# Stage one of the six last batches of an FFT mixing layer: split float32r products in place of float32 ones

## The chip, the cores and the metric

The kernel runs on one core of a Trainium2 chip. The metric is the device time of one execution in microseconds (us). A NeuronCore has five engines with a queue of instructions each: TensorE (PE, with its weight loads as PEld), VectorE (DVE), ScalarE (ACT), GpSimd (POOL) and SyncE (SP), which here issues most of the DMAs. An engine takes its queue in order; semaphores make it wait for other engines and for DMAs.

## What is computed

`x` has 8 batches of 3008 positions with 256 channels. A real FFT runs over the positions, the spectrum is mixed over the channels with a complex weight matrix and a bias, shrunk softly, and transformed back. A feed-forward block with 2048 hidden units and a squared ReLU follows. All of it is float32.

```python
X = np.fft.rfft(x, axis=1)
Yr = Xr @ w_r - Xi @ w_i + b_r
Yi = Xr @ w_i + Xi @ w_r + b_i
Yr = np.sign(Yr) * np.maximum(np.abs(Yr) - lam, 0.0)      # Yi likewise
y = np.fft.irfft(Yr + 1j * Yi, n=3008, axis=1)
h = np.maximum(y @ w_in, 0.0)
out = (h * h) @ w_out
```

## The kernel before

3008 is 64 x 47, so the FFT is done in two stages. Stage one is a transform of length 47 for each of 64 residues, with the 47 inputs folded into 24 sums and 24 differences: a product with the constant matrix `am32` (120 x 2 x 120), which serves five residues at a time. Thirteen steps of this kind make up a batch, and their results go to memory in `s1`. Stage two and the mixing (class `Pair`), the transform back (`Pair.back`, `Back`) and the feed-forward block (`Tokens`, `Step`) follow.

In the main loop, slot after slot, the feed-forward block of batch `b` runs as the backbone: tiles of about 500 positions, eight `Step`s a tile, two slots a `Step`. Each `Step` makes seven products into `psh` (21 matmuls of 250 columns), lets DVE and ACT turn them into `c`, rounds that to float32r on ACT and forms the rest on POOL (`mg`, two halves), and multiplies `mg` with `wout` into `pso` (two times six matmuls of 500 columns). All of these stand at line 478, the line of a helper (`then`) that ties them into one order on each engine. Beside it run the pairs of batch `b + 1` and stage one of batch `b + 2`, as jobs with a due slot: `fwd_tasks` gives a `Fwd` step every 7 slots (6 in the first round). Its load is due 2.5 slots ahead of the step, `add` 0.8 ahead and `run` 0.3 after.

A `Fwd` step loads `xt` (line 209, two buffers), folds it into `xs` by two POOL instructions (lines 212 and 227, one buffer), and `run` (line 232) multiplies: two float32 products of `am32` with 256 columns (line 235), an ACT copy into `xe`, and a store. This is how batches 2 to 7 go, six of them, 78 steps. Batch 0 is done by `Fwd32` at the start (line 367) and batch 1 by `Fwd2` (line 346), which needs no folds but a third weight matrix, `nam`, the negative of half of `am32`.

`halves(hi, lo, v, eng)` is the helper of every split: `hi` is `v` rounded to float32r by a copy on ACT (line 97), `lo` the rest `v - hi` in float32r, subtracted on `eng` (line 101). A product of two split operands is three float32r matmuls: high by high, low by high, high by low, as in `Pair.mul` (line 300).

Tiles are taken by name with a number of buffers from `FRONT` and `MAIN`, two where neither says otherwise. A new tile waits for all readers of the one whose buffer it takes. `SIDE` lists the tiles that lie in the memory that becomes free once the weights are converted, in slot 5. The order of the instructions of an engine is not that of the program: it is laid out ahead of the run from expected times, with the due slots as the order of preference; `issue_after` ties one instruction behind another. `load_next` chains the loads of `xt`, `ka`, `kb` and `du` on SP in this way.

Of the kernel before, what the change touches and what calls it, by code (L numbers as in the profile page):

```python
# [9 lines left out]
F32 = mybir.dt.float32  # L10
F32R = mybir.dt.float32r
# [12 lines left out]
B, S, D, FF = 8, 3008, 256, 2048  # L24
# [4 lines left out]
M1 = R * G  # L29
# [8 lines left out]
}  # L38
MAIN = {
    "xs": 1, "xe": 1, "du": 1, "kv": 1, "kp": 1, "kq": 1, "ksh": 1, "ksl": 1, "kxl": 1, "kb": 1, "yr": 1,  # L40
    "ms": 1, "mp": 1, "mu": 1, "mv": 1, "mc": 3, "nam": 1,
}
CONV = ("big", "small", "dw", "ds")
SIDE = ("xs", "ka", "kb", "kcm", "kxh", "kxl", "kp", "kq", "ke", "kv", "ksh", "ksl", "kuh", "kul", "ku")

# [11 lines left out]
def fnet_moe(ctx: ExitStack, tc, x, w_r, w_i, b_r, b_i, w_in, w_out, bm, cm, dx, a32, c32, out):  # L59
    nc = tc.nc  # L60
    pe, act, dve, pool = nc.tensor, nc.scalar, nc.vector, nc.gpsimd
# [7 lines left out]
    am32 = const.tile([M1, 2, M1], F32, name="am32")  # L69
# [11 lines left out]
    def memory(stack, name, **kwargs):  # L81
        return stack.enter_context(tc.tile_pool(name=name, bufs=2, reuse_waits="tile", **kwargs))
# [5 lines left out]
    def T(name, shape, dt, tag=None):  # L88
        tag = tag or name
        return pools.get(tag, phase["pool"]).tile(shape, dt, name=name, tag=tag, bufs=phase["bufs"].get(tag, 2))  # L90

    def bank(shape, name="psf"):
        return phase["psum"].tile(shape, F32, name=name, tag=name, bufs=phase["bufs"].get(name, 1))

    def copy(eng, out, in_):
        if eng is act:
            return act.copy(out=out, in_=in_)  # L97
        return eng.tensor_copy(out=out, in_=in_)  # L98

    def sub(eng, out, a, b):  # L100
        return eng.tensor_tensor(out=out, in0=a, in1=b, op=ALU.subtract)  # L101
# [65 lines left out]
    def halves(hi, lo, v, eng):  # L167
        copy(act, hi, v)
        sub(eng, lo, v, hi)
# [33 lines left out]
    class Fwd:  # L203
# [19 lines left out]
            )  # L223
            return nc.sync.dma_start(dst, self.ev[:, :n])


        def add(self):
            self.u = T("xs", [M1, 2, D], F32)
            for t in range(2):
                self.fold(pool, self.u[:, t:t + 1], t)  # L230

        def run(self):
            ps = bank([128, 2, D])
            for t in range(2):
                nc.tensor.matmul(ps[:M1, t], am32[:, t], self.u[:, t], start=True, stop=True)  # L235
            self.ev = T("xe", [M1, 1, 2, D], F32)
            copy(act, self.ev[:, 0], ps[:M1])
            self.store()
# [99 lines left out]
    class Fwd2(Fwd):  # L338
# [3 lines left out]
        def run(self):  # L342
            ps = bank([128, 2, D])
            for t in range(2):
                for i in range(2):
                    nc.tensor.matmul(  # L346
                        ps[:M1, t], nam if t and i else am32[:, t], self.xt[:, 0, i], start=i == 0, stop=i == 1
                    )
            self.ev = T("xe", [M1, 1, 2, D], F32)
            copy(act, self.ev[:, 0], ps[:M1])  # L350
            self.store()
# [230 lines left out]
    def pair_tasks(pairs, start, step):  # L582
        jobs = []
        for j, u in enumerate(pairs):
            at = start + j * step
            if j:
                jobs += [(at - 3.7, u.load)]
            jobs += [
                (at, u.fwd), (at + 1.0, u.sums), (at + 3.7, u.load_back),
                (at + 2.1, lambda u=u: u.mix(1)), (at + 3.0, lambda u=u: u.mix(0)), (at + 4.0, u.shrink),  # L590
                (at + 7.1, lambda u=u: u.back(0)), (at + 8.0, lambda u=u: u.back(1)),
            ]
        return jobs

    def fwd_tasks(b, start, step):
        jobs = []
        for q in range(J):
            f, at = Fwd(b, q), start + q * step
            jobs += [(at - 2.5, f.load), (at - 0.8, f.add), (at + 0.3, f.run)]
        return jobs  # L600

    def back_tasks(t, start):
        b, c0, h = tiles[t]
        new = range(-(-c0 // W2), -(-(c0 + 2 * h) // W2))
        jobs = []
        for j, q in enumerate(new):
            k, at = Back(b, q), start + 2.2 * j
            jobs += [(at, k.load), (at + 1.6, k.mm)]
            if len(k.spans) > 1:
                jobs += [(start + 14.6, k.put)]  # L610
        k = Tokens(t)
        for j in range(2):
            jobs += [(start + 7.1 + j, lambda j=j: k.sums(j))]
        for j in range(4):
            jobs += [(start + 9.1 + 1.2 * j, lambda j=j: k.split(j))]
        return jobs
# [24 lines left out]
    def convert(n, after=None):  # L641
        p = parts[n]
        p.bits(after)
        p.join()
        if n % 4 > 1:
            p.split()
        elif n % 4:
            win_sums(n // 4, parts[n - 1:n + 1])
# [10 lines left out]
    for r in range(-5, len(units) + 3):  # L659
# [20 lines left out]
        pool=memory(ctx, "main"), bufs={**{k: FRONT[k] for k in CONV}, **MAIN, "psf": 2}, psum=memory(ctx, "main_ps", space=PSUM)  # L680
# [9 lines left out]
                job()  # L690
    for n in range(len(parts) - LATE, min(LATER.values())):
        convert(n, units[-1])
    nam = T("nam", [M1, M1], F32)
    act.mul(nam, am32[:, 1], -1.0)
    second = [Fwd2(1, q) for q in range(J)]
    for q in range(3):
        second[q].load()
# [3 lines left out]
    for m in range(2 * len(steps) + 4):  # L701
        b, r = divmod(m, slots)
        if r == 0 and b < B:
            jobs = [(t - slots, job) for t, job in jobs]
            if b + 1 < B:
                first, step = 1.0, 6.1
                if b == 0:
                    first, step = 11.2, 5.5
                    for q in range(2, J):
                        if q > 2:  # L710
                            jobs += [(0.9 * (q - 3), second[q].load)]
                        jobs += [(0.5 + 0.9 * (q - 2), second[q].run)]
                    jobs += [(first - 0.6, pairs[1][0].load)]
                jobs += pair_tasks(pairs[b + 1], first, step)
            if b + 2 < B:
                first, step = (2.6, 7.0) if b else (14.6, 6.0)
                jobs += fwd_tasks(b + 2, first, step) + [(95.0, pairs[b + 2][0].load)]
            for j in range(len(HALF)):
                t = b * len(HALF) + j + 1
                if t < len(tiles):  # L720
                    jobs += back_tasks(t, NF * j + 0.5)
            jobs.sort(key=lambda j: j[0])
        n, k = divmod(m, 2)
        if k and 0 <= n - 2 < len(steps):
            steps[n - 2].out(1)
        if n < len(steps):
            (steps[n].second if k else steps[n].first)()
        if not k and 0 <= n - 2 < len(steps):
            steps[n - 2].out(0)
        if m in LATER:  # L730
            convert(LATER[m], steps[n])
        if m == max(LATER):
            conv.close()
            pools.update(dict.fromkeys(CONV), **dict.fromkeys(SIDE, memory(ctx, "side")))
        while jobs and jobs[0][0] < r + 1:
            jobs.pop(0)[1]()

# [85 lines left out]
```

## Time and profile before

| | us |
|---|---|
| median of 3 runs | 2632.47 |
| the runs | 2632.03 to 2634.69 |
| profiled execution | 2632.53 |
| its span | 2630.8 |
| TensorE busy | 2569.7 |
| VectorE busy | 1781.6 |
| ScalarE busy | 1670.4 |
| GpSimd busy | 1654.5 |

The profile is of one execution. The span goes from its first to its last instruction. The chain of waits is followed back from the last instruction, at each step to what released it. Durations of single matmuls overlap, since the engine starts one before the last has drained, so what a matmul costs is read from the pitch of a row of them in the chain.

### The profile page before, as it was taken

To read this page: it belongs to the slowest core of one execution; us is meant where nothing else is said; L and a number is where in the kernel's file an instruction comes from. 1 tells how busy PE (TensorE), PEld (TensorE's weight loads), DVE (VectorE), ACT (ScalarE), POOL (GpSimd) and SP (SyncE) were. 2 spreads that over 40 slices of the span, in tenths; PEclk is the share of its full clock that TensorE was granted. 3 is DMA by queue.
4 is the path that set the end of the run, shared out by engine and by line. 5 is a ranking of instruction groups with operands and counts; after the bars stand their busy time and mean duration, and the time that the engine had idled before them with its cause. 6 is when DMAs were issued, how large, how long until landed. Compare 5 with 4: busy or idle time off the path is not lost.

```text
span 2630.8 us, 47549 instructions
## 1 busy us (share of the span) xinstructions
PE 2569.7 (98%) x16908; PEld 2349.9 (89%) x16908; DVE 1781.6 (68%) x3797; ACT 1670.4 (63%) x2433; POOL 1654.5 (63%) x1628
## 2 busy tenths in 40 slices
PE   6798989999999999999999999999999999999999
PEld 4688989899999999999999999999999999999998
DVE  6866666676766667677675766767676677765554
ACT  3465656666666666666666666666666666666665
POOL 3245656766676667666675676667766666666564
PEclk8899999999999999999999999999999999999999
DMA  8642333333332333323332333223332223221100
GB/s 261 202 141 88 111 101 94 90 106 93 112 90 78 113 101 96 89 85 104 103 95 84 101 104 103 89 82 99 103 108 87 72 80 93 77 67 39 35 17 17
DMA packets 191455, 250.51 MB, mean 95 GB/s; under 512 B 21755, under 2 KB 135923, under 8 KB 191219
## 3 DMA queue, kind: packets, MB, share of 16 engines
q1 hardware_dynamic: 178915, 225.12, 28.0%
q0 software_dynamic: 12304, 22.35, 3.6%
q8 instruction: 136, 2.23, 0.4%
q14 instruction: 100, 0.82, 0.1%
HBM read 146.85 MB, written 100.53 MB: 94 GB/s over the span
## 4 chain that ended last, share of the span: by engine, by line
PE 91%; DMA 3%; DVE 3%; POOL 2%; ACT 1%; issue 1%; SPq 0%; POOLq 0%; ACTq 0%; DVEq 0%
PE pso L478 38%; PE psh L478 34%; PE psf L300 7%; PE psf L279 3%; PE psf L235 2%; PE psf L332 2%; PE psf L458 1%; PE psf L459 1%; PE psf L455 1%; DMA du<-s 1%; POOL mg L101 1%; PE psf L346 1%; PE psf L409 1%; DMA x<-x_in 0%; DMA s<-xe 0%
## 5 line engine op out<-in xcount | busy, mean ns | idle before, releaser
L101 POOL TENSOR_TENSOR mg<-mc,mg 128x500 fp32r<-128x500 f32 (+1 forms) x768 | 973.8, 1288 | 589.0 <-ACT mg L97 536.0
L478 PE MATMUL pso<-mg,wout 128*128 128x500 f32 (+1 forms) x4608 | 1178.0, 393 | 3.2 <-POOL mg L101 1.7
L478 PE MATMUL psh<-yt,win 128*128 128x250 f32 (+1 forms) x8064 | 1072.4, 281 | 0.0
L478 ACT ACTIVATE mc<-mc 128x1000 f32<-128x1000 f32 (+1 forms) x768 | 802.5, 1045 | 416.0 <-DVE mc L478 406.0
L478 PEld LDWEIGHTS psh<-yt,win 128*128 128x128 f32 x8064 | 1021.9, 189 | 31.8
L478 PEld LDWEIGHTS pso<-mg,wout 128*128 128x128 f32 x4608 | 819.8, 189 | 132.8 <-POOL mg L101 4.3
L478 DVE TENSOR_TENSOR mc<-psh,mv 128x500 f32<-128x500 f32 (+3 forms) x768 | 419.1, 547 | 439.7 <-PE psh L478 407.4
L97 ACT CAST mg<-mc 128x1000 fp32r<-128x1000 f32 (+1 forms) x384 | 396.9, 1034 | 18.2 <-ACT mc L478 0.4
L478 DVE TENSOR_TENSOR mv<-psh,mu 128x500 f32<-128x500 f32 (+1 forms) x384 | 260.6, 679 | 53.9 <-PE psh L478 22.9
L300 PE MATMUL psf<-wx,kxh 128*128 128x256 f32 x1008 | 208.0, 283 | 0.8 <-DVE ke L312 0.8
L98 DVE COPY mp<-psh 128x250 f32<-128x250 f32 (+1 forms) x384 | 159.6, 416 | 40.9 <-PE psh L478 18.6
L101 POOL TENSOR_TENSOR ksl<-kv,ksh 128x512 fp32r<-128x512 f32 x84 | 108.6, 1293 | 107.9 <-ACT ksh L97 107.9
L300 PEld LDWEIGHTS psf<-wx,kxh 128*128 128x128 f32 x1008 | 167.5, 190 | 4.9 <-DVE ke L312 1.3
L478 DVE TENSOR_TENSOR mu<-psh,mp 128x250 f32<-128x250 f32 (+1 forms) x384 | 160.6, 418 | 11.7
L214 POOL TENSOR_TENSOR xs<-xt 120x256 f32<-120x256 f32 x156 | 114.6, 754 | 84.9 <-DMA xt<-x_in 76.7
L321 DVE TENSOR_TENSOR kv<-psf,ke 64x256 f32<-64x256 f32 x336 | 141.8, 422 | 28.1 <-PE psf L300 20.0
L478 DVE TENSOR_TENSOR mc<-psh,mp 128x250 f32<-128x250 f32 (+1 forms) x384 | 156.8, 408 | 5.2 <-PE psh L478 3.6
L300 PE MATMUL psf<-wx,kxl 128*128 128x256 f32 x504 | 141.5, 281 | 0.0
L97 ACT CAST kuh<-psf 128x256 fp32r<-128x256 f32 x192 | 68.3, 372 | 99.5 <-PE psf L332 79.8
L97 ACT COPY dy<-psf 128x188 f32<-128x188 f32 x256 | 76.5, 312 | 86.5 <-PE psf L459 86.2
L312 DVE TENSOR_TENSOR ke<-psf,bias 128x512 f32<-128x512 f32 x84 | 58.0, 691 | 105.8 <-PE psf L300 105.5
L97 ACT CAST ksh<-kv 128x512 fp32r<-128x512 f32 x84 | 52.0, 619 | 114.5 <-DVE kv L101 114.3
(97 smaller groups left out, 2565.4 us busy)
## 6 DMA issues: line engine op xcount, KB each, us to landing
du<-s SPq DMA_DIRECT2D x128, 256.0 KB, 2.9
s<-kuh SPq DMA_DIRECT2D x192, 128.0 KB, 1.8
s<-kul SPq DMA_DIRECT2D x192, 128.0 KB, 1.9
s<-xe SPq DMA_DIRECT2D x92, 240.0 KB, 2.4
xt<-x_in SPq DMA_DIRECT2D x91, 240.0 KB, 3.4
kcm<-cm_in POOLq DMA_DIRECT2D x84, 256.0 KB, 3.3
ka<-s SPq DMA_DIRECT2D x84, 256.0 KB, 3.4
du<-s SPq DMA_DIRECT2D x256, 64.0 KB, 2.7
```

What stands on the lines that cost most here:

```text
L97: return act.copy(out=out, in_=in_)
L98: return eng.tensor_copy(out=out, in_=in_)
L101: return eng.tensor_tensor(out=out, in0=a, in1=b, op=ALU.subtract)
L214: return eng.tensor_tensor(out=out[:, :n], in0=self.xt[:, :n, 0], in1=self.xt[:, :n, 1], op=(ALU.add, ALU.subtract)[t])
L235: nc.tensor.matmul(ps[:M1, t], am32[:, t], self.u[:, t], start=True, stop=True)
L279: nc.tensor.matmul(pv[:, :, c, g, :], self.a[:, g, c * 128:(c + 1) * 128], bg, start=True, stop=True)
L300: self.last = nc.tensor.matmul(ps, l, wx[j][:, k, c, :], start=n == 0, stop=n == 5)
L312: dve.tensor_add(out=self.e, in0=self.pe, in1=bias)
L321: dve.tensor_add(out=v[64 * r:64 * r + 64, g], in0=ps[gs], in1=self.e[gs, r])
L332: nc.tensor.matmul(ps[:, :D], self.cm[:, g, j * 128:(j + 1) * 128], r[:, g], start=n == 0, stop=n == 2)
L346: nc.tensor.matmul(ps[:M1, t], nam if t and i else am32[:, t], self.xt[:, 0, i], start=i == 0, stop=i == 1)
L478: last_of[eng] = op(*args, **kwargs)
```

## The change

`Fwd.add` splits the folded sums `u` into `uh` and `ul` by `halves`, with POOL for the subtraction; both take the tag `xt`, that is the two buffers that the loads use. `Fwd.run` makes three float32r matmuls for each half `t` instead of a float32 one. `am32` is split once, in slot 5, into `amh` (in the `SIDE` memory) and `aml`, which takes the buffer of `nam`; `nam` gets the shape of `aml` for that. `Fwd2` and `Fwd32` compute as before.

```diff
 MAIN = {
     "xs": 1, "xe": 1, "du": 1, "kv": 1, "kp": 1, "kq": 1, "ksh": 1, "ksl": 1, "kxl": 1, "kb": 1, "yr": 1,
-    "ms": 1, "mp": 1, "mu": 1, "mv": 1, "mc": 3, "nam": 1,
+    "ms": 1, "mp": 1, "mu": 1, "mv": 1, "mc": 3, "nam": 1, "amh": 1,
 }
-SIDE = ("xs", "ka", "kb", "kcm", "kxh", "kxl", "kp", "kq", "ke", "kv", "ksh", "ksl", "kuh", "kul", "ku")
+SIDE = ("xs", "ka", "kb", "kcm", "kxh", "kxl", "kp", "kq", "ke", "kv", "ksh", "ksl", "kuh", "kul", "ku", "amh")
         def add(self):
-            self.u = T("xs", [M1, 2, D], F32)
+            u = T("xs", [M1, 2, D], F32)
             for t in range(2):
-                self.fold(pool, self.u[:, t:t + 1], t)
+                self.fold(pool, u[:, t:t + 1], t)
+            self.uh = T("xh", [M1, 2, D], F32R, tag="xt")
+            self.ul = T("xl", [M1, 2, D], F32R, tag="xt")
+            halves(self.uh, self.ul, u, pool)
         def run(self):
             ps = bank([128, 2, D])
             for t in range(2):
-                nc.tensor.matmul(ps[:M1, t], am32[:, t], self.u[:, t], start=True, stop=True)
+                for n, (a, u) in enumerate(((amh, self.uh), (aml, self.uh), (amh, self.ul))):
+                    nc.tensor.matmul(ps[:M1, t], a[:, t], u[:, t], start=n == 0, stop=n == 2)
-                        ps[:M1, t], nam if t and i else am32[:, t], self.xt[:, 0, i], start=i == 0, stop=i == 1
+                        ps[:M1, t], nam[:, 0] if t and i else am32[:, t], self.xt[:, 0, i], start=i == 0, stop=i == 1
-    nam = T("nam", [M1, M1], F32)
-    act.mul(nam, am32[:, 1], -1.0)
+    nam = T("nam", [M1, 2, M1], F32)
+    act.mul(nam[:, 0], am32[:, 1], -1.0)
         if m == max(LATER):
             conv.close()
             pools.update(dict.fromkeys(CONV), **dict.fromkeys(SIDE, memory(ctx, "side")))
+            amh, aml = (T(name, [M1, 2, M1], F32R, tag=tag) for name, tag in (("amh", "amh"), ("aml", "nam")))
+            halves(amh, aml, am32, pool)
```

## Rows read from the trace of the kernel before

**Rows 1.** The page, busy us (share of the span) and instructions of each engine
```profile
PE 2569.7 (98%) x16908; PEld 2349.9 (89%) x16908; DVE 1781.6 (68%) x3797; ACT 1670.4 (63%) x2433; POOL 1654.5 (63%) x1628
```

**Rows 2.** Stretches of the span: busy us (instructions) of each engine, clock, DMA
```profile
core 0: us, PE busy (x) PEld busy (x) DVE busy (x) ACT busy (x) POOL busy (x), PEclk, DMA share, GB/s
300.00:400.00 100.00, 92.97 (x620) 85.72 (x619) 66.80 (x145) 58.74 (x90) 61.77 (x65) 0.97 0.38 110
...
600.00:800.00 200.00, 199.97 (x1340) 184.16 (x1339) 135.73 (x290) 131.60 (x191) 135.78 (x138) 1.00 0.34 99
...
1400.00:1600.00 200.00, 199.48 (x1346) 183.90 (x1345) 135.24 (x291) 127.47 (x182) 135.61 (x136) 1.00 0.32 92
```

**Rows 3.** TensorE's waits, whole span: us in total, times, longest us
```profile
PE pso L478 <- POOL mg L101: 1.7, 2, 1.2
PE pso L478 <- ACT mg L97: 1.3, 1, 1.3
```

**Rows 4.** TensorE's waits from 200 to 600 us
```profile
PE psf L332 <- ACT ksh L97: 10.9, 2, 6.5
```

**Rows 5.** Chain of waits, pieces of four stretches: start us, us, what
```profile
710.59 1.41 PE psf L300 x12
...
933.90 0.89 PE psf L279 x8
934.79 0.87 PE psf L235 x4
...
935.90 2.25 PE pso L478 x10
...
954.61 0.86 PE psf L235 x4
...
1018.05 0.24 PE psf L332 x2
```

**Rows 6.** Groups by line: shapes, count, busy us, mean ns, idle before
```profile
L101 POOL TENSOR_TENSOR ksl<-kv,ksh 128x512 fp32r<-128x512 f32 x84 | 108.6, 1293 | 107.9 <-ACT ksh L97 107.9
L235 PEld LDWEIGHTS psf<-xs,am 120*120 120x120 f32 x312 | 52.9, 182 | 7.2
L300 PEld LDWEIGHTS psf<-wx,kxh 128*128 128x128 f32 x1008 | 167.5, 190 | 4.9 <-DVE ke L312 1.3
L97 ACT CAST ksh<-kv 128x512 fp32r<-128x512 f32 x84 | 52.0, 619 | 114.5 <-DVE kv L101 114.3
```

**Rows 7.** Tile `xs`: duration ns, first and last start; engines idle before them
```profile
L235 PE MATMUL psf<-xs,am x312: 377/378/397, 199.9 to 2038.0; 120*120 120x256 f32 x156
...
  DMA xt<-x_in: 76.7, 43
  issue: 7.2, 1
  DVE ke L312: 0.9, 1
```

**Rows 8.** ACT's instructions in order of time, 924 to 938 us: start, us
```profile
931.74 1.04 ACT L97 CAST mg<-mc 128x1000 fp32r<-128x1000 f32 x1
...
934.07 0.61 ACT L97 CAST yt<-ms 128x500 fp32r<-128x500 f32 x1 [0.78 <-POOL ms L101]
```

**Rows 9.** POOL's instructions in order of time, 924 to 938 us
```profile
930.06 1.45 POOL L214 TENSOR_TENSOR xs<-xt 120x256 f32<-120x256 f32 x2 [1.75 <-DMA xt<-x_in]
931.47 1.29 POOL L101 TENSOR_TENSOR ksl<-kv,ksh 128x512 fp32r<-128x512 f32 x1
...
934.00 2.45 POOL L101 TENSOR_TENSOR mg<-mc,mg 128x500 fp32r<-128x500 f32 x2
```

**Rows 10.** SP's DMA issues in order of time, 935 to 960 us
```profile
950.96 0.54 SPq L108 DMA_DIRECT2D xt<-x_in  x1
```

**Rows 11.** The page, DMA issues: count, KB each, us to landing
```profile
xt<-x_in SPq DMA_DIRECT2D x91, 240.0 KB, 3.4
```

**Rows 12.** Tile `nam`, the products that read it: duration ns, first and last start
```profile
L346 PE MATMUL psf<-xt,nam x26: 379/379/379, 129.5 to 183.6; 120*120 120x256 f32 x26
```

## What the change will do to the time

> **What bounds the kernel now.** I read the page's engine table first: TensorE is busy 98% of the span and the next engine 68%, so time is won or lost on TensorE alone [rows 1]. Busy time is no proof of that, since ends of matmuls are modelled; so the stretches come next. In each of the five stretches of 200 us from 600 to 1600 us, of which the first and the last are shown, TensorE is busy over 199 us, at a granted clock of 1.00, the upper level of 2.4 GHz, while POOL and ACT are busy some 136 and 130 us; from 300 to 400 us it is busy 93 of 100, at 0.97 [rows 2]. Then its waits: in the whole span it waited 1.7 us for POOL's and 1.3 us for ACT's results of the big products [rows 3], and between 200 and 600 us 10.9 us for ACT's `ksh` [rows 4]. The reader is to see that in the middle of the kernel a matmul that becomes shorter pulls in everything behind it, and that no other engine holds it up as yet.
>
> **What is removed.** The chain of waits gives the pitch, not the modelled duration. At line 235 there are 78 steps of two products; each product shows as two records, and four records (one step) take 0.86 to 0.87 us [rows 5], so a float32 product of 256 columns costs 0.433 us. There are 156 of them: 312 records, 156 of them with the form 120x256 [rows 7]. They cost 156 x 0.433 = 67.5 us on the path.
>
> **What takes their place.** Three float32r products each, 468 in all. The trace of before has no float32r product with weights 120 columns wide. The nearest rows are line 300's, float32r with 256 moving columns and a weight load for each of them: 12 in 1.41 us, 0.1175 us each [rows 5]. Line 332's, of the same shape, take 0.12 us [rows 5]. At the other end stands the rate of the float32 product itself, which streams its 256 columns four times in 0.433 us: 0.108 us a pass. So a triple costs 0.324 to 0.360 us, and by line 300, which is nearest in type, width and change of weights, 0.3525 us. The gain is 156 x (0.433 - 0.3525) = 12.6 us, with ends 156 x 0.073 = 11.4 us and 156 x 0.109 = 17.0 us.
>
> A page speaks against this. Line 300's row shows that a weight load for every product adds at most 0.1175 - 0.108 = 0.010 us to it. The Trainium skill, TensorE: Matmul & The Clock Gate, Part 3, says that a weight load runs beside a matmul in flight only where the row groups differ, which they don't here. By its figure for a load (columns over 1.2 GHz, so about 0.100 us for 120 columns, an estimate from that page's section on LDWEIGHTS) a triple would cost some 0.62 us and the change would lose about 30 us. The trace disagrees with that by a wide margin; the sum goes by the row.
>
> **What ACT and POOL get.** Each of the 78 steps adds a rounding copy of 120 x 512 on ACT, as the `ksh` copy, 0.62 us, and a subtraction of the same size on POOL, as `ksl`, 1.29 us [rows 6]: 48 and 101 us over the span. The steps lie between 199.9 and 2038 us, one every 23.6 us [rows 7]. In that time POOL is idle some 7.6 us (64 of 200) and ACT some 8.2 us (70 of 200) [rows 2]. With the 1.28 us that POOL idles for the copy ahead of an average `ksl` (107.9 / 84) [rows 6], a step takes 2.57 us of POOL and 0.62 us of ACT. It fits, and costs nothing by load; what it costs by delay is the question.
>
> The delay: the rounding copy sits in ACT's queue and must wait for POOL's two folds, which wait for the load of `xt` (76.7 us over 43 of the 156 folds, 1.8 us each) [rows 7]. Behind it on ACT stand relu, square and copy of the next step of the big products, behind POOL's new subtraction that step's two `mg` halves, and TensorE's line 478 waits for both. The room is read from one step: ACT's `mg` copy ends at 932.78 and the twelve output products start at 935.90, 3.1 us later [rows 5, 8]. POOL's first half ends at about 935.2 (half of 2.45 us from 934.00) [rows 9], and the fifth product, the first to read it, starts near 935.90 + 4 x 0.225 = 936.8, 1.6 us later. The new subtraction (1.29) fits into 1.6; with a wait for the copy it does not always. The trace has a like case without harm: POOL's `ksl` stood between the folds and these `mg` halves, and ACT idled 0.78 us for POOL ahead of a `yt` copy [rows 8, 9]. The order of instructions on each engine is not the program's but worked out from expected times, so most of these new ones will lie in gaps. I take 0.04 us a step, 3 us in all; between 0 (TensorE waits as little as now) and 0.5 us at each of the 43 late folds, 21 us (the slower rival below). Nothing below zero: the work is only added.
>
> **Buffers and queues.** `xt` has two buffers, now for three tiles. The next load of `xt` can't go before the products of the step before have read both parts. Today it sometimes does: one load is issued at 950.96 and the products of the step before run from 954.61 [rows 5, 10]. Loads on SP's queue are chained in order, so `du`, `ka` and `kb` behind it would shift by 3.5 us and more there. What covers it: a step has 23.6 us [rows 7], and load (3.4 us to landing [rows 11]), wait, folds (1.45 [rows 9]), copy, subtraction and triples need some 3.4 + 1.8 + 1.45 + 0.62 + 2.57 + 0.7 = 10.5 us. I cost it at nothing; without the cover, a late tile of the big products is priced below. `xs` is freed by the subtraction instead of the products, which only helps. The two parts of `am32` are made once, in less than the 0.62 and 1.29 us above since they have 240 columns, off the path, and one of them in `nam`'s buffer, so after `nam`'s last reader.
>
> Sum: the profiled execution took 2632.53 us (span 2630.8, 1.7 around it), the median is 2632.47, so both scales agree. 2632.5 - 12.6 + 3 = 2623 us.
>
> **Rivals.** Faster still: the 120-column triple runs near the stream rate, and waits don't grow: 2632.5 - 17.0 = 2615.5, up to 2620. For it: the float32 product with the same weights shape adds under 2 ns a pass to 256 / 2.4 = 106.7; against it: both float32r rows [rows 5].
>
> Given back: the same gain, but 0.1 us and more lost per step (8 to 14 us) as ACT stands behind late folds: 2627 to 2637.
>
> Slower, by ACT's new wait: at a late fold ACT is held for 1.8 + 1.45 = 3.2 us, about its room of 3.1, and POOL then starts its `mg` halves 1.29 + 0.62 = 1.9 us later against a room of 1.6 [rows 7, 8, 9]. If neither finds cover, TensorE loses near 0.5 us at each of 43 late folds, 21 us: 2632.5 - 12.6 + 21 = 2641. It decides from 12.6 / 78 = 0.16 us a step on. Against it: the same folds hold POOL as long today, and TensorE waits for `mg` 1.7 us in all [rows 3].
>
> Slower, by loads: if each of the six batches has one tile late by 3 us because `du` stands behind an `xt` that waits, 18 us are lost: 2638.
>
> Slower, by the weight load: the nearest 120-column loads, float32, come one per 0.216 us [rows 5]. Should a float32r load of 120 columns need as much, a triple would cost 0.648 us and the change 156 x 0.215 = 34 us: 2666. Against it: line 279 loads 128 float32 columns every 0.111 us (8 in 0.89) [rows 5]. The same page of the Trainium skill, under Weight-path perf modes, has the fast load only at 128 weights of a type other than float32. Line 300's loads of 128 columns last 0.190 us and line 235's float32 ones of 120 columns 0.182 [rows 6], so the trace shows no faster kind to be lost.
>
> The change not doing what it says: POOL's subtraction into `nam`'s buffer is queued early and POOL stands until the last products with `nam`, which are spread from 129.5 to 183.6 us [rows 12]; of these 54 us perhaps 30 would be lost, an estimate without a nearer row. Against it: `xs` has one buffer that products free, and no fold was ever found waiting for them [rows 7]; the order is chosen so that this doesn't happen.
>
> **How the numbers follow.** The forecast case (2620 to 2627) 0.50; faster still 0.14; given back 0.18; slower by ACT's wait 0.11; by loads 0.04; by weight load or `nam` 0.03. Faster by over 0.2% (5.3 us, about what a measurement of this kernel can tell from no change) means below 2627.2: 0.50 + 0.14 = 0.64; within it 0.18; slower 0.18. The range runs from 2612 (the 17 us gain, and 3 us for an early part that is laid out anew, where 10.9 us are waited now) to 2640, which takes in most of the given-back case and part of the slower one.
>
> **What would show it.** Right: line 235 with 468 products, six of them in 0.70 us of the chain; TensorE still busy 199 of 200 us from 600 to 1600; waits of line 478 for `mg` under 6 us; batches shorter by 13 x 2 x 0.08 = 2.1 us each. Wrong in the sum: a step of six at 0.65 us or at 1.2 us. Wrong in the delay: new rows of TensorE waiting for `mg` or for `uh` and `ul`, ACT idle for POOL's `xs` over 1 us a step. Wrong in the queue: TensorE waiting for `du`, or for `yt`, at the start of a tile.

## The result, and the profile after

| | median, us | runs, us |
|---|---|---|
| before | 2632.86 | 2628.34 to 2634.69 (18) |
| after | 2636.43 | 2631.05 to 2643.60 (18) |

The ratio is 1.0016, 95% interval 1.0009 to 1.0023. The kernel became slower by some 4 us: less than the 5.3 us that was set as the bound of "no change", but beyond its interval, and on the other side of the forecast (2623 us). The profiled execution of after has a span of 2632.1 us, 1.3 more than before.

The page, the engines (compare [rows 1]):

```profile
PE 2564.6 (97%) x17064; PEld 2349.7 (89%) x17064; DVE 1822.7 (69%) x3797; ACT 1710.8 (65%) x2512; POOL 1758.7 (67%) x1707
```

TensorE's busy time fell by 5 us while its waiting grew. ACT and POOL got 40 and 104 us more of busy time, as the split demands (79 more instructions on each). The number to stop at is DVE's: not one instruction more than before (3797), and yet 41 us more busy. The 84 clamps of the shrink step (DVE, line 326) took 27 us of that, the 84 subtractions behind them (`kv<-kv,kc`) 12 us.

The products themselves. Pieces of the chain of waits (start us, us, what), from stretches around 627 and 943 us, beside [rows 5]:

```profile
628.62 1.79 PE pso L481 x8
...
632.15 0.71 PE psf L238 x6
...
943.52 0.70 DVE kv L101
...
944.25 0.63 ACT ksh L97
...
944.92 0.68 PE psf L335 x2
945.60 3.19 PE pso L481 x8
```

Six float32r products take 0.71 us, 0.118 us each, where four float32 records took 0.86 to 0.87. So a step saves 0.155 us, and 78 of them 12.1 us. The other rows show what became of it. Ahead of the two products of line 335 (332 before) the chain runs through DVE and ACT instead of TensorE, and the eight `pso` products behind them take 3.19 us there, 1.79 us elsewhere.

TensorE's waits from 400 to 2100 us (us in total, times, longest):

```profile
PE psf L335 <- ACT ksh L97: 10.0, 6, 2.1
PE psf L458 <- DMA du<-s: 2.7, 7, 0.6
PE psf L282 <- DMA kb<-bm_in: 0.5, 1, 0.5
```

In the kernel before, TensorE waited 2.6 us in all in this stretch: 1.4 for `du` and 1.2 for `mg`. Now there are 13.2 us, and 10.0 of them are the transform back (line 335) waiting for `ksh`. It is one wait a batch, of 1.7 to 2.1 us in five batches, always at the same place of the batch, and 0.3 us once more. In the early part (200 to 400 us) the same wait shrank, from 10.9 us [rows 4] to 4.1, but others grew there: all waits listed for this part fell from 13.6 to 9.7 us.

Stretches of the span with the granted clock (the last three figures: clock, DMA share, GB/s). The first three answer to [rows 2], the others are short ones:

```profile
300.00:400.00 100.00, 96.93 (x672) 90.03 (x671) 74.39 (x149) 65.92 (x99) 71.88 (x72) 1.00 0.37 110
...
600.00:800.00 200.00, 197.54 (x1349) 182.28 (x1348) 139.40 (x284) 131.97 (x193) 146.50 (x144) 1.00 0.32 93
...
1400.00:1600.00 200.00, 197.79 (x1343) 182.58 (x1342) 139.48 (x289) 130.56 (x190) 145.18 (x142) 0.99 0.31 92
...
945.10:948.50 3.40, 3.40 (x10) 2.81 (x11) 3.00 (x7) 3.19 (x5) 1.12 (x1) 0.50 0.04 12
...
1261.00:1264.40 3.40, 1.48 (x8) 1.31 (x9) 3.09 (x7) 1.74 (x3) 1.50 (x2) 1.00 0.30 96
...
1580.10:1583.30 3.20, 3.20 (x12) 2.78 (x11) 2.24 (x5) 3.17 (x6) 0.29 (x2) 0.50 0.00 0
1897.50:1900.70 3.20, 3.20 (x10) 2.61 (x9) 2.82 (x6) 3.16 (x5) 0.95 (x1) 0.50 0.00 0
```

After three of the five waits (those that end at 944.9, 1579.0 and 1897.1 us) TensorE's clock was at the lower level, 1.2 GHz (0.50), for over 3 us. This is why the eight `pso` products took 1.4 us longer. After the waits that end at 628 and 1263 us it stayed up. From 300 to 400 us, in turn, the clock rose from 0.97 to 1.00 and TensorE's busy time from 93 to 97 us: the early part came out better than before.

Now the cause of the late `ksh`. One of the five places, DVE, POOL and ACT in order of time (start us, us, engine, line, out<-in, idle time before it):

```profile
936.90 1.73 DVE L324 TENSOR_TENSOR kv<-psf,ke 64x256 f32<-64x256 f32 x4
938.66 4.82 DVE L326 TENSOR_SCALAR kc<-kv 128x512 f32<-128x512 f32 x1
943.52 0.69 DVE L101 TENSOR_TENSOR kv<-kv,kc 128x512 f32<-128x512 f32 x1
```

```profile
938.23 1.29 POOL L101 TENSOR_TENSOR xl<-xs,xh 120x512 fp32r<-120x512 f32 x1
939.48 2.46 POOL L101 TENSOR_TENSOR mg<-mc,mg 128x500 fp32r<-128x500 f32 x2
941.90 0.27 POOL L474 COPY yr<-dy 128x120 f32<-128x120 f32 x1
942.14 1.06 POOL L101 TENSOR_TENSOR yt<-ms,yt 128x500 fp32r<-128x500 f32 x1
944.94 1.28 POOL L101 TENSOR_TENSOR ksl<-kv,ksh 128x512 fp32r<-128x512 f32 x1 [1.74 <-ACT ksh L97]
```

```profile
944.25 0.62 ACT L97 CAST ksh<-kv 128x512 fp32r<-128x512 f32 x1 [5.90 <-DVE kv L101]
```

DVE's clamp of `v` into `kc` (line 326, 323 before) took 4.82 us. The shortest of its kind take 0.42. POOL meanwhile worked through five instructions that follow one another without a gap, from 938.23 to 943.20 us, and the clamp ended at 943.48, just behind the last. The first of the five is the new subtraction `xl`. The same clamp in the kernel before, the seventh of the twelve of the same batch, and POOL beside it:

```profile
950.23 0.43 DVE L323 TENSOR_SCALAR kc<-kv 128x512 f32<-128x512 f32 x1
```

```profile
946.14 2.47 POOL L101 TENSOR_TENSOR mg<-mc,mg 128x500 fp32r<-128x500 f32 x2
951.91 2.96 POOL L101 TENSOR_TENSOR mg<-mc,mg 128x500 fp32r<-128x500 f32 x2 [3.30 <-DVE mu L478]
```

There the clamp fell into a gap of 3.30 us between POOL's instructions and took its shortest time. All clamps, before and after (tile `kc`: shortest, median, longest in ns, first and last start):

```profile
L323 DVE TENSOR_SCALAR kc<-kv x84: 416/560/4382, 206.7 to 2306.2; 128x512 f32<-128x512 f32 x84
```

```profile
L326 DVE TENSOR_SCALAR kc<-kv x84: 417/782/4824, 206.3 to 2308.6; 128x512 f32<-128x512 f32 x84
```

So the theory (A) that the experiments had to test: **DVE's clamp does not get started while POOL's instructions follow one another without a gap; the new subtraction closes a gap, and TensorE pays at line 335.** The rivals: the load buffers that the parts now share (B), a merely unlucky order of instructions (C), and ACT's new wait, on which the forecast had put its delay.

As a general rule the first half of the theory is too strong, and the trace of after shows it. Here a clamp ends in the middle of a pair of `mg` halves that follow each other directly (DVE, then POOL):

```profile
855.43 1.41 DVE L326 TENSOR_SCALAR kc<-kv 128x512 f32<-128x512 f32 x1
```

```profile
855.27 2.69 POOL L101 TENSOR_TENSOR mg<-mc,mg 128x504 fp32r<-128x504 f32 x2 [5.07 <-ACT mg L97]
```

It ended at 856.84 us, 0.28 behind the first half, and the second half took 1.45 us in place of 1.26. Of the 84 clamps of after, 16 took under 0.5 us, 57 ended just behind the first POOL instruction that they met (39 of them although the next one followed at once), and 11 stood through two to five, the five above among them. In the six traces with the clamp in SBUF (before, after, `e3`, `e5`, `e6`, `e10`), 53 of the 111 clamps of 0.5 us and more that had their own subtraction directly behind them on DVE stood through more than one POOL instruction, and 8 of the 209 others. No run tests whether that order on DVE is the reason.

### The profile page after: what moved, and what is told of

It reads as the page before. It is cut to its first block, busy times and chain, and to the rows that moved or that the text cites. A ratio compares the mean times of both kernels' runs of the same rounds, so it can differ in the third digit from the quotient of the medians.

```text
span 2632.1 us, 47984 instructions
## 1 busy us (share of the span) xinstructions
PE 2564.6 (97%) x17064; PEld 2349.7 (89%) x17064; DVE 1822.7 (69%) x3797; ACT 1710.8 (65%) x2512; POOL 1758.7 (67%) x1707
## 4 chain that ended last, share of the span: by engine, by line
PE 85%; DVE 6%; DMA 4%; issue 1%; ACT 1%; POOL 1%; SPq 0%; POOLq 0%; ACTq 0%; DVEq 0%
PE pso L481 36%; PE psh L481 32%; PE psf L303 7%; PE psf L282 2%; PE psf L335 2%; PE psf L238 2%; DMA du<-s 1%; DVE kc L326 1%; DMA s<-xe 1%; PE psf L461 1%; PE psf L462 1%; PE psf L458 1%; DVE kv L101 1%; DVE kv L324 1%; POOL mg L101 1%
## 5 line engine op out<-in xcount | busy, mean ns | idle before, releaser
L468 DVE TENSOR_TENSOR yr<-psf,dy 128x188 f32<-128x188 f32 (+4 forms) x256 | 77.9, 312 | 63.5 <-ACT dy L97 58.1
```

The source lines that it names most:

```text
L468: dve.tensor_add(out=o, in0=ps[:, 0, lo:hi], in1=y[:, c, lo:hi])
```

## The experiments

Each was timed against the kernel before on the same chip; ratios have a 95% interval.

**The clamp out of POOL's way.** `e1` writes the clamp into the PSUM bank of the product that it follows; the rest of the changed kernel stays, buffers included.

```diff
-            ps = bank([128, 512])[:, :D]
+            pb = bank([128, 512])
+            ps = pb[:, :D]
             self.mul(ps, 2)
-            cl = T("kc", [128, 2, D], F32, tag="ke")
+            cl = pb.rearrange("p (g d) -> p g d", g=2)
```

> The changed kernel, with the clamp of the shrink step (line 326, DVE) written into the PSUM bank of its product instead of SBUF. Theory A (the clamp can't run while POOL's instructions follow one another without a gap; the new subtraction closes such a gap, the clamp takes 4.7 us, ksh is late and TensorE waits 2 us once a batch and then loses its clock for 3.4 us): every clamp takes under 0.8 us, line 335 waits under 3 us in all after 400 us, the clock stays at the upper level from 400 us on, and the time is 2618 us, within 4. Rival B (parts in the loads' buffers make du late): du waits stay near 12 us and the time stays at 2633 to 2637. Rival C (the order laid out anew is merely worse): no telling, 2625 to 2640.

Measured: 2626.61 us, ratio 0.9976 (0.9968 to 0.9985), 10 us under the changed kernel's 2636.43. The clamps (tile `kv`), and TensorE's waits from 400 to 2100 us:

```profile
L327 DVE TENSOR_SCALAR psf<-kv x84: 681/684/697, 208.3 to 2298.8; 128x512 f32<-128x512 f32 x84
```

```profile
PE psh L482 <- POOL yt L101: 4.6, 6, 1.2
PE pso L482 <- POOL mg L101: 1.0, 4, 0.5
...
PE psf L459 <- DMA du<-s: 0.3, 1, 0.3
```

All 84 clamps take 0.68 to 0.70 us whatever POOL does, and the wait of the transform back is gone from this stretch. Rival B falls as the cause of the late transform back: the parts are still in the loads' buffers, and `du` is waited for 0.3 us. But the time is 2627, not 2618: a new wait stands in the place of the old one, TensorE for POOL's `yt` at the start of a tile, 4.6 us. POOL's queue is longer by the subtraction for that too. That puts the time outside theory A's range (2614 to 2622) and inside the wide one of rival C. The edit also leaves the clamp without a buffer of `ke`; the next run has that too and gains nothing by it.

**The same edit without the change.** `e2` is the kernel before with this diff.

> The kernel before, float32 products, with the same clamp in PSUM. Theory A: the kernel before has clamps of 2.2 to 2.7 us in its middle that no one waits for, and one of 4.4 us and one of 2.3 us in its early part where line 332 then waits 4.4 and 6.5 us; so 2622 to 2632, and e1 lies some 12 us below this run. Rival C: 2628 to 2637, and the distance to e1 need not be 12.

Measured: 2633.63 us, ratio 1.0002 (0.9993 to 1.0011). By itself the edit brings nothing, since in the middle of the kernel before no one waits for a long clamp. Theory A had expected a gain in the early part (2622 to 2632); the time lies above that, in rival C's range. TensorE's waits listed from 200 to 400 us fell from 13.6 to 10.2 us, but early in the next block the clock was at the lower level (0.50 from 482.7 to 489.3 us, where the kernel before has 1.00). The 7.0 us between `e2` and `e1`, timed side by side, are what the whole change is worth once the clamp is out of the way: not 12.

**No subtraction on POOL.** In `e3` the third product of each triple reads the high part once more, so the low part of the sums is left out.

```diff
-            self.ul = T("xl", [M1, 2, D], F32R, tag="xt")
-            halves(self.uh, self.ul, u, pool)
+            copy(act, self.uh, u)
-                for n, (a, u) in enumerate(((amh, self.uh), (aml, self.uh), (amh, self.ul))):
+                for n, (a, u) in enumerate(((amh, self.uh), (aml, self.uh), (amh, self.uh))):
```

> The changed kernel without POOL's subtraction; the third product of each triple reads the high part again, so the low part of the sums is left out. Six products a step as before this edit. Theory A: POOL keeps its gaps, the 4.7 us clamps go, 2621 us within 5. Rival (ACT's rounding copy behind the folds is what holds TensorE): the copy is still there, 2632 to 2637. Rival B (buffers): uh still sits in a buffer of the loads, 2630 to 2637.

Measured: 2623.52 us, ratio 0.9964 (0.9950 to 0.9977). TensorE's waits from 400 to 2100 us:

```profile
PE psf L457 <- DMA du<-s: 1.1, 2, 0.7
PE pso L480 <- POOL mg L101: 0.9, 1, 0.9
PE psf L334 <- ACT ksh L97: 0.5, 1, 0.5
```

With the copy on ACT and the six products in place, 2.8 us of waits are left, about as in the kernel before (2.6), and the forecast's time comes out. ACT's copy costs nothing that shows, so the rival with ACT's new wait falls; the subtraction on POOL, in the changed kernel's order, is what cost 13 us. The edit also takes `xl` out of the loads' buffers, but those were not the cause in `e1`.

**The split without its use.** `e6` is the other half: copy and subtraction stay, the products are float32 again.

```diff
-            u = T("xs", [M1, 2, D], F32)
+            self.u = u = T("xs", [M1, 2, D], F32)
-                for n, (a, u) in enumerate(((amh, self.uh), (aml, self.uh), (amh, self.ul))):
-                    nc.tensor.matmul(ps[:M1, t], a[:, t], u[:, t], start=n == 0, stop=n == 2)
+                nc.tensor.matmul(ps[:M1, t], am32[:, t], self.u[:, t], start=True, stop=True)
```

> The kernel before with the split added (rounding copy on ACT, subtraction on POOL, both parts in the buffers of the loads) but not used: the products stay float32, two a step. Theory A: the price of the split alone on top of the float32 products, 2632 + 10 to 15 = 2642 to 2647. Rival (the products' gain never reached the path): 2633 to 2637, the same as the changed kernel.

Measured: 2648.87 us, ratio 1.0061 (1.0049 to 1.0074): 15 us over the kernel before and 12.4 over the changed one. The place of the loss is not that of the changed kernel: from 400 to 2100 us `e6` waits 1.0 us for `ksh` and 5.8 in all, and some 11 of its 15 us arise early: the feed-forward block's second batch begins at 492 us, in the kernel before at 481. The agreement of 12.4 with 12.1 is luck, and `e6` does not show that the products' gain is on the path. The starts of the feed-forward blocks, read from the first `psh` product of each batch, tell this (us; 65 of the 78 steps lie between the start of the second block and that of the seventh):

| | second block starts | from there to the seventh | span |
|---|---|---|---|
| before | 480.9 | 1580.2 | 2630.8 |
| after | 473.7 | 1589.7 | 2632.1 |
| `e1` | 476.2 | 1576.7 | 2623.0 |
| `e2` | 477.7 | 1585.3 | 2633.3 |
| `e3` | 479.7 | 1572.8 | 2621.8 |
| `e6` | 492.3 | 1586.4 | 2647.1 |

In these five blocks `e6` is 3.3 us shorter than after, in spite of its float32 products; what it loses against after lies ahead of them. That the gain reaches the path is shown by `e3` and `e1`: of the 10.1 us that 65 steps save, `e3` is 7.4 us shorter there than before, and `e1` 8.6 us shorter than `e2`. `e6` also has the same run of five POOL instructions, subtraction first, beside the seventh clamp of the batch, but there the clamp starts 4.4 to 4.7 us into the run (0.4 to 0.8 in after) and takes 0.54 to 0.86 us. So what the run costs depends on when the clamp comes.

**The subtraction on DVE.** `e5` frees POOL by giving the subtraction to DVE, the clamp in SBUF as in the changed kernel.

```diff
-            halves(self.uh, self.ul, u, pool)
+            halves(self.uh, self.ul, u, dve)
```

> The changed kernel with the subtraction of the low part on DVE instead of POOL. Theory A (POOL's subtraction closes the gaps that DVE's clamp needs): POOL's queue is as before, no clamp of over 4 us after 400 us, line 335 waits under 3 us there, and the time is 2620 to 2627. Rival (the extra work as such holds the chain from products to ksh, whoever does it): DVE gets 78 times 0.7 us and makes ksh or kv as late as POOL did, 2631 to 2640.

Measured: 2671.19 us, ratio 1.0149 (1.0135 to 1.0163), the slowest of all; both numbers expected were too low. DVE and POOL in order of time, then TensorE's waits in the whole span:

```profile
1273.51 6.74 DVE L101 TENSOR_TENSOR xl<-xs,xh 120x512 fp32r<-120x512 f32 x1
1280.17 0.41 DVE L98 COPY mp<-psh 128x250 f32<-128x250 f32 x1
```

```profile
1273.82 1.08 POOL L101 TENSOR_TENSOR yt<-ms,yt 128x500 fp32r<-128x500 f32 x1
1274.85 4.85 POOL L101 TENSOR_TENSOR mg<-mc,mg 128x500 fp32r<-128x500 f32 x4
```

```profile
PE psf L282 <- DVE ke L315: 24.3, 5, 5.2
```

The clamps are short now, none over 2.8 us, and after 400 us line 335 has no wait for `ksh` of over 0.3 us: this half of the theory held. But the subtraction, whose two inputs both lie in SBUF, is caught in the same way. It stood from 1273.51 to 1280.25 us behind a DMA issue and five instructions of POOL without a gap, and DVE's `ke` behind it held TensorE for some 5 us in each of five batches. On average it took 1.54 us. DVE's `kxl`, as large but with one input in PSUM, takes 0.69. So it is not the clamp as such, but a DVE instruction that needs something POOL holds. The seventh clamp, 4.4 to 4.8 us in five batches of after, takes 0.43 here and 1.18 in `e3`.

**Both, or half of each.** `e7` joins `e1` and `e5`; `e8` is `e1` with the sums subtracted on POOL and the differences on DVE.

```diff
-            halves(self.uh, self.ul, u, pool)
+            copy(act, self.uh, u)
+            for t, eng in enumerate((pool, dve)):
+                sub(eng, self.ul[:, t], u[:, t], self.uh[:, t])
```

> Both: the clamp in PSUM and the subtraction on DVE. e1 had no late ksh any more, but TensorE waited 6.5 us for POOL's yt at the start of tiles. Theory A with POOL's queue as the second cost: with the subtraction off POOL these waits go too, batches take 313 to 314 us (315.3 in the kernel before) and the time is 2616 to 2623. Rival: DVE's queue becomes late in turn, 2624 to 2632.

> e1 (clamp in PSUM) with the subtraction divided: the half of the sums on POOL, the half of the differences on DVE. In e1 TensorE waited 6.5 us for POOL's yt at the start of tiles, about 1.1 us a batch. Theory (POOL's subtraction has two prices, the clamp and the late yt): with half of it on POOL the waits for yt shrink below 3 us, 2620 to 2626. Rival (DVE pays as much as POOL saves, as in e7): 2627 to 2631.

Measured: `e7` 2629.39 us, ratio 0.9989 (0.9980 to 0.9998); `e8` 2659.73 us, 1.0095 (1.0079 to 1.0110). In `e7` the waits from 400 to 2100 us fall to 5 us, with none for `yt` over 0.2, and still `e1` is faster: the time is in the rival's range (DVE late in turn). DVE's `xl` took up to 2.9 us; where the rest goes wasn't found. In `e8` TensorE's waits are, in the whole span:

```profile
PE psf L338 <- ACT ksh L97: 15.2, 5, 3.5
...
PE psf L284 <- DVE ke L317: 6.8, 4, 4.9
...
PE psh L484 <- POOL yt L101: 1.9, 2, 1.1
```

The wait for `yt` shrank as expected, but the half on DVE, 256 columns, takes 1.17 us on average and up to 7.3, and what stands behind it on DVE is late instead: 27 us lost, which neither theory had in its numbers.

**Another order.** `e10` is the changed kernel with folds and split due 1.6 slots ahead, `e9` is `e1` with the tokens' sums and splits due 0.8 slots earlier.

```diff
-            jobs += [(at - 2.5, f.load), (at - 0.8, f.add), (at + 0.3, f.run)]
+            jobs += [(at - 2.5, f.load), (at - 1.6, f.add), (at + 0.3, f.run)]
```

```diff
-            jobs += [(start + 7.1 + j, lambda j=j: k.sums(j))]
+            jobs += [(start + 6.3 + j, lambda j=j: k.sums(j))]
-            jobs += [(start + 9.1 + 1.2 * j, lambda j=j: k.split(j))]
+            jobs += [(start + 8.3 + 1.2 * j, lambda j=j: k.split(j))]
```

> The changed kernel with the same instructions, but folds and split due 1.6 slots ahead of the step instead of 0.8, so that the order on the engines is laid out anew. Rival C (an unlucky order, no more): the time changes with what happens to stand beside the clamps, 2622 to 2632, and the 4.7 us clamps at one place of each batch go or move. Theory A alone, with the subtraction always beside a clamp: 2633 to 2639, the 4.7 us clamps stay.

> e1 with the sums and splits of the tokens (ms, yt) due 0.8 slots earlier, all of the subtraction on POOL. Theory (yt is late because POOL's queue is fuller, a matter of order): the waits for yt vanish and batches take 313 to 314.5 us, 2620 to 2625. Rival (POOL's added work delays mg instead, or du is not there so early): 2625 to 2632.

Measured: `e10` 2636.34 us, ratio 1.0015 (1.0006 to 1.0023), the changed kernel's time again. Its clamps:

```profile
L326 DVE TENSOR_SCALAR kc<-kv x84: 417/822/4784, 206.2 to 2310.8; 128x512 f32<-128x512 f32 x84
```

The long clamps and the five waits of 1.9 to 2.1 us at the same place of the batch are there with this due time too, so the loss doesn't hang on the first order alone. Rival C is not gone, though: in the order of `e6`, with the same work on POOL, none of the five long clamps occurs. `e9` gave 2625.26 us, ratio 0.9971 (0.9960 to 0.9983), the fastest version that computes everything, and faster than both kernels. Its wait for `yt` only fell from 4.6 to 4.0 us, so the reason given for it did not hold; that it beats `e1` isn't shown, since the intervals overlap.

## Why the prediction was wrong

**What bounds the kernel** was right, and with it the weight of every microsecond of waiting. The measured time lies in the range of the rival "given back" (2627 to 2637), but by luck: that rival had ACT behind late folds as its mechanism.

**The products** were right. 12.6 us were predicted from line 300's pitch; the chain of after gives 12.1. Float32r loads of 120 columns go at the pitch of the 128-column ones, 0.118 us a product. The rule of the Trainium skill (TensorE: Matmul & The Clock Gate, Part 3) by which a load overlaps with a matmul in flight only where the row groups differ does not hold for this kernel's products. Their loads (`psf<-xl,amh`) are busy for 0.180 to 0.187 us each, and one product follows the other every 0.118 us.

**POOL's and ACT's time** was right in size: 101.7 us of `xl` and 48.1 of `xh` were predicted as 101 and 48. "It fits, and costs nothing by load" was the sentence that failed. POOL's idle time was counted as free room. Some of it was in use: the clamp that took 0.43 us before ran in such a gap, and beside POOL's full queue it took 4.82. The profile before showed it to whoever looked at DVE, which the prediction did not do, since the change adds no DVE instruction. The clamps of line 323 took between 0.416 and 4.382 us there.

**The delay** was priced at 3 us and looked for at the wrong place. It came to some 16 us: 2636.4 against 2632.9 less the 12.1 of the products. Copy behind folds on ACT, `mg` late on POOL: TensorE waited for `mg` 1.5 us in all in the profile after (3.0 before [rows 3]), so that mechanism, and the slower rival built on it, did not occur. What occurred stood in no rival. In the profiled execution it comes to some 10.6 us of added waits from 400 to 2100 us (13.2 against 2.6), and three stretches of over 3 us at half the clock, which at the 1.4 us seen on eight `pso` products in the one come to at least 4.2 us. In the five blocks of the table, the steps save 10.1 us (65 x 0.155), yet the blocks became 9.5 us longer: 19.6 us were lost there. The waits and the clock make some 15 of them; the rest was not itemised. The signs that the prediction had set say the same: TensorE is busy 197.5 and 197.8 of 200 us, not 199, and a batch is 1.9 us longer, not 2.1 shorter.

**Buffers and queues**: costed at nothing. TensorE's wait for `du` from 400 to 2100 us rose by 1.3 us (2.7 against 1.4), and `e1`, with the same buffers, has 0.3. That was right. In the whole span the wait for `du` rose from 5.5 to 12.4 us, but 5.9 of that is one wait ahead of 200 us, where the kernel before and `e1` wait 5.8 us for DVE's `dw` instead. The rival on `nam`'s buffer did not occur: no wait on it shows.

**The early part** was given 3 us either way. It gained more than that here (7.2 us up to the second block) and lost some 11 us in `e6`: how an order turns out there is not foreseen from the rows.

**The spread.** After has runs from 2631 to 2644 us, twice the spread of before. That the clock falls after some of the 2 us waits and not after others would make such a spread, but only one execution was profiled, so this is argued and not shown. The mean clock of each run bears it out only weakly: 0.993 in the fastest, but 0.991 both at 2633.8 and at 2643.6 us.

## What to carry to other kernels

Before work is put into an engine's idle time, ask which other engine uses that idle time: compare the shortest and the longest duration of one and the same instruction on the neighbours, and see what the first engine did during the long ones. Here one instruction varied tenfold with no change in its shape, because it waited for something that POOL held, and the wait was booked as busy time. Where DVE's elementwise work must stand beside a dense POOL queue, and something waits for it, try an operand or its output in PSUM: that took 10 us off the changed kernel, and nothing off the kernel before, where no one waited.

## What the runs showed of the hardware

A clamp from SBUF to SBUF on DVE (one tensor in, one out, 128 x 512 float32) takes 0.42 us at best, and 4.8 us beside five POOL instructions without a gap; a subtraction with both inputs in SBUF took 6.7 us in the same way. With the result in PSUM the same clamp took 0.68 to 0.70 us in all 84 cases: slower than the best, and never held. The Trainium skill, SBUF — State Buffer, under "Who interferes with whom", says that a DVE instruction in one of the modes that use two ports, which a `tensor_scalar` such as the clamp can enter, or with two inputs in SBUF contends with GpSimd for a shared pair of ports, and that whoever issues first has the pair for its whole instruction while the other blocks. The trace agrees as to who interferes: in after the clamps took 0.417 to 4.824 us and the subtractions `kv<-kv,kc` of the same size 0.673 to 4.301, but `kxl`, with one input in PSUM, 0.675 to 0.694 in all 84 cases.

The runs add how long a wait can become. Most held clamps got their turn behind the first POOL instruction, in 39 of 57 cases of after between two that follow one another directly. But 11 stood through more, and the five that decided here stood through the instruction that they met and four others.
